# Hard-swish gates on GpSimd, later crossbar transposes and earlier weight loads in a fused top-k attention and feed-forward kernel

## The chip, the core and the metric

The kernel runs on one core of a Trainium2 chip. A core has five engines, each with a queue of its own that is worked off strictly in order: TensorE (PE in the profile; PEld is its weight load), VectorE (DVE), ScalarE (ACT), GpSimd (POOL) and SyncE (SP, which here only issues DMAs). An instruction waits on semaphores for what it needs from other engines, and while it waits, everything behind it on the same engine waits too. The metric is the device time of one execution in microseconds, lower is better; the figure of a kernel is the median of its runs.

## What is computed

Attention over 8 batches of 8 heads with 576 positions and 64 channels, in which each query keeps only its 32 largest scores; then a feed-forward block with a hard-swish between its two products, over the 4608 rows of all batches.

```python
scores = scale * np.matmul(q, k.transpose(0, 1, 3, 2))
kth = np.partition(scores, -top_k, axis=-1)[..., -top_k:-top_k + 1]     # top_k = 32
scores = np.where(scores >= kth, scores, -1000000000.0)
attn = np.exp(scores - np.max(scores, axis=-1, keepdims=True))
attn = attn / (np.sum(attn, axis=-1, keepdims=True) + 1e-09)
x = heads_joined(np.matmul(attn, v))                                    # 4608 x 512
h = x @ w_in                                                            # 512 x 2048
g = h * np.clip(h + 3.0, 0.0, 6.0) / 6.0
return g @ w_out                                                        # 2048 x 512
```

The feed-forward weights are float64 in memory; the kernel reads their raw words and makes float32 of them itself.

## The kernel before

**Attention, in duos.** The heads of a batch form four pairs, and two pairs at a time, for one tile of 128 queries, form a `Duo`. A batch has eight full duos (four query tiles, two halves of the heads) and two rest duos (the last 64 queries of each head): ten per batch, 80 in all. The main loop (L491) goes over them. A duo has two units, u = 0 and u = 1, one for each pair, and each unit of a full duo has two rows of tiles of 128 x 576 scores (a rest duo one). For each unit, VectorE finds the 32 largest scores of every query in four rounds (`top`, L238): MAX8 gives the next eight, MATCH_REPLACE8 strikes them out for the next round. `top(0)` to `top(3)` in the loop are the rounds of unit 0, `top(4)` to `top(7)` those of unit 1.

**What follows a unit's rounds.** `exp` (L254): GpSimd makes `kth`, the negated 32nd score, and a shift; ScalarE masks by a very steep Prelu (L265) and takes Exp with a running sum `den` (L270); GpSimd adds a constant to `den` (L275). `weights` (L277): VectorE inverts `den` (L284), GpSimd scales the scores (L287) and splits the float32 words into 16-bit halves, `e16` (L296). Then, still in `weights`, SP issues a transposing DMA of `e16` into `t16` (L299). `join` (L301): ScalarE puts the halves together into `eT` (L305). `values` (L313): TensorE multiplies by v, ScalarE copies the result into `xT` (L332). `exp(0)` and `weights(0)` of a duo come in its own step of the loop, `exp(1)` and `weights(1)` in the next, `join(0)` and `join(1)` in the next, `values` in the one after that. The scores of a duo are made one step ahead (`scores`, L195).

**Feed-forward, in pieces.** When the attention of 128 or 256 rows is complete, `queue` (L420) puts a `feed_forward` generator (L336) into `todo`. It is worked off in pieces between the steps of attention: a piece is either half of one 512-wide block of h (L349), at whose end ScalarE takes Relu(h + 3) into g (L357), or two products towards the output (L370), the last of which is followed by ScalarE's scaling by 1/6 (L380) and SP's store (L382). The gate, min(g, 6) * h, is one VectorE instruction (L361). It reads h from PSUM, and `piece` (L403) issues it two pieces after the piece that made g. The PSUM pool `ps_w` has three buffers for h, for the attention values and for the output sums; `ps_big` has one for scores and transposed inputs. At four places in each step (after rounds 0, 1, 3 and 5) `piece` is called with a count that depends on whether the duo is a rest duo and on the backlog `left`, in pieces (L496 to L500).

**Weights.** `convert` (L94) loads 128 x 512 raw float64 words into `st` (L100), then ScalarE (L105, L108), GpSimd (L106, L119) and VectorE (L114, L115) make float32 of them. There are 32 such chunks. `convert_step` (L462) is called after every round while chunks are left: it finishes an older chunk, then issues the load of the next one and starts on it at once.

**Buffers and queues.** The pool `kq` has 14 buffers of 4.6 KB per partition. Inputs as they land, transposed k and q, `st`, `e16`, `t16` and `eT` all come from it. Everything that SP issues goes through one queue, in the order of the program: input loads (L147, L151), values (L159, L163), weights (L100), transposes (L299) and stores (L382). The order is written out by hand; nothing reorders it.

Of the kernel before, what the change touches and what calls it, by code (L numbers as in the profile page):

```python
# [9 lines left out]
ALU = mybir.AluOpType  # L10
F32 = mybir.dt.float32
U32 = mybir.dt.uint32
I32 = mybir.dt.int32
U16 = mybir.dt.uint16
# [14 lines left out]
def kernel(  # L29
# [9 lines left out]
    nc = tc.nc  # L39
    P = nc.NUM_PARTITIONS  # L40
    B, H, S, D = q.shape
    DM, FF = moe_w_in.shape
    J = S // P
# [8 lines left out]
    def pool(name, bufs, **kw):  # L52
        return ctx.enter_context(tc.tile_pool(name=name, bufs=bufs, **kw))

    consts = pool("consts", 1)
    kqpool = pool("kq", 14)
    scpool = pool("sc", 3)
    wkpool = pool("wk", 1)
    mpool = pool("m", 4)
    xtpool = pool("xt", 2)  # L60
    xrpool = pool("xr", 1)
    gpool = pool("g", 8)
    opool = pool("o", 1)
    ps_big = pool("ps_big", 1, space=PSUM)
    ps_w = pool("ps_w", 3, space=PSUM)
# [28 lines left out]
    def convert(dst, src):  # L94

        st = kqpool.tile([P, 2 * WC], U32, tag="kq", name="st")
        nc.sync.dma_start(st[:], src)  # L100
        words = st[:].rearrange("p (n two) -> p n two", two=2)
        lo, hi = words[:, :, 0], words[:, :, 1]
        a = gpool.tile([P, WC], F32, tag="g", name="a")
        y = gpool.tile([P, WC], F32, tag="g", name="y")
        nc.scalar.activation(a[:], hi.bitcast(F32), AF.Abs)  # L105
        nc.gpsimd.tensor_scalar(a[:], a[:], HI_MOST, HI_LEAST, ALU.min, ALU.max)  # L106

        nc.scalar.activation(y[:], lo, AF.Copy, bias=2.0, scale=2.0**-51)  # L108
        yield

        au, yu = a[:].bitcast(U32), y[:].bitcast(U32)
        nc.vector.tensor_scalar(au, au, 3, None, ALU.logical_shift_left)  # L114
        nc.vector.scalar_tensor_tensor(  # L115
            out=yu, in0=hi, scalar=0x80000000, in1=yu,
            op0=ALU.bitwise_and, op1=ALU.bitwise_or,
        )
        nc.gpsimd.tensor_tensor(  # L119
            dst.bitcast(I32), a[:].bitcast(I32), y[:].bitcast(I32), ALU.add  # L120
        )
# [13 lines left out]
    class Pair:  # L135


        def __init__(self, b, hp):
            self.b, self.hp = b, hp
            self.vm, self.vr, self.kr = vms[hp], vrs[hp], krs[b % 2 * NHP + hp]  # L140
# [40 lines left out]
    class Duo:  # L181
# [6 lines left out]
        def __init__(self, pairs, qt):  # L188
            self.pairs, self.qt = pairs, qt
            self.rest = qt == J  # L190
            self.nt = 1 if self.rest else 2
            self.nb = J + 2 if self.rest else 2 * J + 1
            self.t16, self.eT = [None] * 2, [None] * 2

        def scores(self, us=(0, 1)):  # L195

# [80 lines left out]
        def weights(self, u):  # L277

            d = self.den[:, u, 0 : self.nt]
            nc.vector.reciprocal(d, d)  # L284
            for t in range(self.nt):
                row = self.row(u, t)
                nc.gpsimd.tensor_scalar(  # L287
                    row, row, self.den[:, u, t : t + 1], 1.0, ALU.mult, ALU.mult
                )
            n = self.nb * P  # L290
            e16 = kqpool.tile([P, 2 * (2 * J + 1) * P], U16, tag="kq", name="e16")
            halves = e16[:, 0 : 2 * n].rearrange("p (h x) -> p h x", h=2)
            parts = [(0, S + R, 0), (S - P, S, S + R)] if self.rest else [(0, n, 0)]
            for c0, c1, to in parts:
                words = self.sc[:, u, c0:c1].bitcast(U16).rearrange("p (x h) -> p h x", h=2)
                nc.gpsimd.tensor_copy(halves[:, :, to : to + c1 - c0], words)  # L296
            t16 = kqpool.tile([P, 2 * (2 * J + 1), P], U16, tag="kq", name="t16")
            self.t16[u] = t16
            nc.sync.dma_start_transpose(t16[:, 0 : 2 * self.nb, :], e16[:, 0 : 2 * n])  # L299

        def join(self, u):  # L301

# [33 lines left out]
    def feed_forward(xT, nt, rows):  # L336

        gs = []
        nf = 512 // nt
        for f0 in range(0, NFC, nf):
            h = ps_w.tile([P, 512], F32, tag="w", name="h")
            for f in range(f0, f0 + nf):
                if f == f0 + nf // 2:
                    yield None
                for i in range(NHP):
                    nc.tensor.matmul(  # L349
                        h[:, (f - f0) * nt : (f - f0 + 1) * nt],  # L350
                        w_in[:, i, f * P : (f + 1) * P],
                        xT[:, i, 0:nt],
                        start=(i == 0),
                        stop=(i == NHP - 1),
                    )
            g = gpool.tile([P, 512], F32, tag="g", name="g")
            nc.scalar.activation(g[:], h[:], AF.Relu, bias=three[:], scale=1.0)  # L357
            gs.append(g)

            def gate(g=g, h=h):  # L360
                nc.vector.scalar_tensor_tensor(  # L361
                    out=g[:], in0=g[:], scalar=6.0, in1=h[:], op0=ALU.min, op1=ALU.mult
                )

            yield gate
        for t0 in range(0, nt, P):
            acc = ps_w.tile([P, DM], F32, tag="w", name="acc")
            for f in range(NFC):
                c0 = f % nf * nt + t0
                nc.tensor.matmul(  # L370
                    acc[:],
                    gs[f // nf][:, c0 : c0 + P],
                    w_out[:, f, :],
                    start=(f == 0),
                    stop=(f == NFC - 1),
                )
                if f % 2 == 1:
                    if f == NFC - 1:
                        o = opool.tile([P, DM], F32, tag="o", name="o")
                        nc.scalar.mul(o[:], acc[:], 1.0 / 6.0)  # L380
                        for p0, p1, dst in rows(t0):
                            nc.sync.dma_start(dst, o[p0:p1, :])  # L382
                    yield None
# [16 lines left out]
    left = 0  # L400
# [56 lines left out]
            queue(state["xT"], c0 + P, rows)  # L457

    chunks = list(weight_chunks())
    converting = []  # L460

    def convert_step(depth=1):  # L462

        while len(converting) > depth:
            next(converting.pop(0), None)
        if converting and not chunks:
            next(converting.pop(0), None)
        if chunks:
            c = convert(*chunks.pop(0))
            next(c)  # L470
            converting.append(c)

    def pair_at(m, first):

# [2 lines left out]

    first = pairs[0]
    first[0].load()
    convert_step(2)  # L480
    first[0].transpose()
    duos[0].scores((0,))
    first[1].load()
    convert_step(2)
    first[1].transpose()
    duos[0].scores((1,))
    first[2].load()
    convert_step(2)
    first[3].load()

    for m in range(ND + 2):  # L491
        u = duos[m] if m < ND else None
        prev = duos[m - 1] if 0 < m <= ND else None


        level = (left >= 10) + (left >= 20)  # L496
        if u and u.rest:
            count = [(1, 0, 1, 0), (1, 0, 1, 1), (1, 1, 1, 1)][level]
        else:
            count = [(2, 1, 2, 1), (2, 2, 2, 1), (2, 2, 2, 2)][level]  # L500
        depth = 2 if m < 2 else 1

        def top(r):
            if u:
                u.top(r // 4, r % 4)
            convert_step(depth)

        if prev:
            prev.exp(1)
        elif m == 0:  # L510
            first[2].transpose()
            first[3].transpose()
        if m + 1 < ND:
            duos[m + 1].scores()
        top(0)
        piece(count[0])
        p = pair_at(m, 4)
        if p:
            p.load()
        if m == 0:  # L520
            first[0].load_values()
            first[1].load_values()
        top(1)
        if prev:
            prev.weights(1)
        if m > 1:
            values(m - 2)
        if u and u.pairs[0].b and 1 <= m % per_batch <= 2:
            for p in duos[m - 1].pairs:
                p.load_values()  # L530
        piece(count[1])
        top(2)
        if prev:
            prev.join(0)
        top(3)
        if u:
            u.exp(0)
        if m == 0:
            first[2].load_values()
            first[3].load_values()  # L540
        piece(count[2])
        top(4)
        p = pair_at(m, 5)
        if p:
            p.transpose()
        top(5)
        if u:
            u.weights(0)
        piece(count[3])
        top(6)  # L550
        if prev:
            prev.join(1)
        top(7)
        if m == 3:
            piece(3)
    while todo:
        piece()
    piece(2)
# [33 lines left out]
```

## Time and profile before

| | |
|---|---|
| Median of three runs | 1792.3 us (1792.1 to 1793.2) |
| The profiled execution | 1793.5 us, of which its instructions span 1791.7 us |
| Granted TensorE clock, mean over the span | 0.923 |
| MAX8 and MATCH_REPLACE8 on VectorE, mean of one | 744 and 740 ns |
| The gate L361 on VectorE | 144 times, 96.7 us, 106.4 us of idle time before it |
| Relu L357 on ScalarE | 144 times, 97.1 us |
| Matmuls towards h (L349) and towards the output (L370) | 474.8 us for 2304 records, 523.4 us for 1152 |
| Transposing DMA L299, issue to landing | 160 times, 4.6 us |
| Weight load L100, issue to landing | 32 times, 5.2 us |

In the profile a line such as `L361 DVE SCALAR_TENSOR_TENSOR g<-g,h` names the line of the kernel, the engine, the operation and what it writes and reads; then come shapes, count, busy time, mean time of one, and the time for which the engine stood idle just before, with what ended the wait. A float32 matmul leaves two records. In a timeline, the first column is the start in us from the beginning of the span and the second the time taken; `SPq` is SP's queue, where the time is that from the first issue to the last of a merged row.

### The profile page before, as it was taken

To read this page: it belongs to the slowest core of one execution; us is meant where nothing else is said; L and a number is where in the kernel's file an instruction comes from. 1 tells how busy PE (TensorE), PEld (TensorE's weight loads), DVE (VectorE), ACT (ScalarE), POOL (GpSimd) and SP (SyncE) were. 2 spreads that over 40 slices of the span, in tenths; PEclk is the share of its full clock that TensorE was granted. 3 is DMA by queue.
4 is the path that set the end of the run, shared out by engine and by line. 5 is a ranking of instruction groups with operands and counts; after the bars stand their busy time and mean duration, and the time that the engine had idled before them with its cause. 6 is when DMAs were issued, how large, how long until landed. Compare 5 with 4: busy or idle time off the path is not lost.

```text
span 1791.7 us, 24696 instructions
## 1 busy us (share of the span) xinstructions
PE 1502.2 (84%) x8480; PEld 986.7 (55%) x8480; DVE 1560.9 (87%) x3249; ACT 1190.7 (66%) x1639; POOL 735.2 (41%) x1218
## 2 busy tenths in 40 slices
PE   5122767697999999899999899899999899998999
PEld 2012454464665656464756656565666565555575
DVE  3856899999999989999999989999999999999310
ACT  4354687777877777678777777777766877766410
POOL 2565444434444444444344444434443434444100
PEclk9555888799999999999999999999999999999999
DMA  6323343444344433535244442444244533323200
GB/s 184 90 92 121 90 100 63 80 85 92 71 82 88 92 83 54 102 78 109 49 79 90 80 88 49 108 86 91 54 101 82 92 64 73 83 54 70 46 13 12
DMA packets 450302, 144.23 MB, mean 80 GB/s; under 512 B 433280, under 2 KB 441472, under 8 KB 450176
## 3 DMA queue, kind: packets, MB, share of 16 engines
q1 hardware_dynamic: 450176, 142.65, 37.9%
q8 instruction: 67, 1.10, 0.3%
q14 instruction: 59, 0.48, 0.1%
HBM read 45.09 MB, written 9.44 MB: 30 GB/s over the span
## 4 chain that ended last, share of the span: by engine, by line
DVE 64%; PE 14%; ACT 12%; POOL 3%; issue 3%; DMA 3%; SPq 0%; ACTq 0%; POOLq 0%
DVE m L245 32%; DVE wk L249 26%; PE acc L370 7%; DVE g L361 4%; PE h L349 4%; ACT eT L305 3%; ACT sc L270 3%; ACT sc L228 2%; PE big L222 2%; ACT sc L265 2%; PE pv L325 1%; DMA st<-in_moe_w_out_dram 1%; DMA t<-e 1%; DMA st<-in_moe_w_in_dram 1%; POOL a L106 1%
## 5 line engine op out<-in xcount | busy, mean ns | idle before, releaser
L245 DVE MAX8 m<-wk 128x8 f32<-128x576 f32 x864 | 612.5, 744 | 2.0
L370 PE MATMUL acc<-w_out,g 128*128 128x512 f32 x1152 | 523.4, 602 | 6.2 <-DVE g L361 6.2
L349 PE MATMUL h<-xT,w_in 128*128 128x256 f32 (+1 forms) x2304 | 474.8, 364 | 33.6 <-DVE g L361 22.2
L349 PEld LDWEIGHTS h<-xT,w_in 128*128 128x128 f32 x2304 | 402.6, 195 | 90.9 <-issue 19.1
L305 ACT COPY eT<-t 128x2304 uint16<-128x2304 uint16 (+1 forms) x160 | 418.4, 2615 | 39.6 <-DMA t<-e 39.3
L249 DVE MATCH_REPLACE8 wk<-m,wk 128x576 f32<-128x576 f32 x576 | 423.1, 740 | 0.0
L265 ACT ACTIVATE sc<-sc,kth 128x576 f32<-128x576 f32 x288 | 209.1, 768 | 252.3 <-POOL kth L260 252.2
L370 PEld LDWEIGHTS acc<-w_out,g 128*128 128x128 f32 x1152 | 213.2, 192 | 240.0 <-issue 229.3
L296 POOL COPY e<-sc 128x2304 uint16<-128x2304 uint16 (+1 forms) x192 | 321.2, 1683 | 10.1
L287 POOL TENSOR_SCALAR sc<-sc,den 128x576 f32<-128x576 f32 x288 | 214.7, 754 | 269.4 <-DVE den L284 263.9
L325 PE MATMUL pv<-eT,vm 128*64 128x128 f32 (+1 forms) x2560 | 182.2, 285 | 127.2 <-ACT eT L305 87.6
L325 PEld LDWEIGHTS pv<-eT,vm 128*64 128x64 f32 x2560 | 148.1, 148 | 178.0 <-ACT eT L305 93.0
L270 ACT ACTIVATE sc<-sc,shift 128x576 f32<-128x576 f32 x288 | 219.2, 762 | 3.0
L275 POOL TENSOR_SCALAR den<-den 128x2 f32<-128x2 f32 (+1 forms) x160 | 35.5, 222 | 446.8 <-ACT sc L270 446.8
L245 DVE MAX8 m<-sc 128x8 f32<-128x576 f32 x288 | 203.3, 742 | 15.6 <-ACT sc L231 15.6
L249 DVE MATCH_REPLACE8 wk<-m,sc 128x576 f32<-128x576 f32 x288 | 211.5, 740 | 0.0
L222 PE MATMUL big<-kq 64*128 64x512 f32 x512 | 144.0, 685 | 73.9 <-ACT kr L179 34.6
L361 DVE SCALAR_TENSOR_TENSOR g<-g,h 128x512 f32<-128x512 f32 x144 | 96.7, 672 | 106.4 <-ACT g L357 106.2
L357 ACT ACTIVATE g<-h,three 128x512 f32<-128x512 f32 x144 | 97.1, 681 | 88.0 <-PE h L349 87.8
L222 PEld LDWEIGHTS big<-kq 64*128 64x128 f32 x512 | 48.6, 206 | 142.0 <-issue 46.4
L228 ACT COPY sc<-big 128x2048 f32<-128x2048 f32 (+1 forms) x65 | 118.4, 1822 | 11.2 <-PE big L225 10.9
L260 POOL TENSOR_SCALAR kth<-m 128x2 f32<-128x2 f32 (+1 forms) x160 | 36.5, 228 | 116.9 <-DVE m L245 116.4
(45 smaller groups left out, 996.6 us busy)
## 6 DMA issues: line engine op xcount, KB each, us to landing
landed<-in_k_dram SPq DMA_DIRECT2D x64, 128.0 KB, 2.8
landed<-in_q_dram SPq DMA_DIRECT2D x64, 128.0 KB, 2.9
st<-in_moe_w_in_dram SPq DMA_DIRECT2D x16, 512.0 KB, 5.2
vm<-in_v_dram SPq DMA_DIRECT2D x64, 128.0 KB, 2.3
st<-in_moe_w_out_dram SPq DMA_DIRECT2D x16, 512.0 KB, 5.2
out_dram<-o SPq DMA_DIRECT2D x32, 256.0 KB, 2.4
t<-e SPq DMA_TRANSPOSE x160, 4.6
landed<-in_k_dram SPq DMA_DIRECT2D x32, 32.0 KB, 2.6
```

The costliest lines, as they stand in the source:

```text
L222: nc.tensor.matmul(banks[:, 2 * i + hh, :], pr.qT[d, qs], pr.kT[d, :])
L245: nc.vector.max(self.m[:, t, 8 * r : 8 * r + 8], self.cur[t])
L249: nc.vector.match_replace(wk, self.m[:, t, 8 * r : 8 * r + 8], self.cur[t], LOWEST)
L265: nc.scalar.activation(row, row, AF.Prelu, bias=kth[:, t : t + 1], scale=1.0, alpha=STEEP)
L270: nc.scalar.activation(row, row, AF.Exp, bias=shift[:, t : t + 1], scale=scale, accum_out=self.den[:, u, t : t + 1],)
L287: nc.gpsimd.tensor_scalar(row, row, self.den[:, u, t : t + 1], 1.0, ALU.mult, ALU.mult)
L296: nc.gpsimd.tensor_copy(halves[:, :, to : to + c1 - c0], words)
L305: nc.scalar.copy(eT[:, 0 : self.nb, :] .rearrange("p c q -> p (c q)") .bitcast(U16) .rearrange("p (x h) -> p h x", h=2), self.t16[u][:, 0 ...
L325: nc.tensor.matmul(pv[hh * D : (hh + 1) * D, u * w : (u + 1) * w], pr.vm[:, hh, c, :] if c < J else pr.vr[:, hh, :], rhs, start=(c == 0), ...
L349: nc.tensor.matmul(h[:, (f - f0) * nt : (f - f0 + 1) * nt], w_in[:, i, f * P : (f + 1) * P], xT[:, i, 0:nt], start=(i == 0), stop=(i == NH ...
L361: nc.vector.scalar_tensor_tensor(out=g[:], in0=g[:], scalar=6.0, in1=h[:], op0=ALU.min, op1=ALU.mult)
L370: nc.tensor.matmul(acc[:], gs[f // nf][:, c0 : c0 + P], w_out[:, f, :], start=(f == 0), stop=(f == NFC - 1),)
```

## The change

Five things are changed.

1. The gate is two GpSimd instructions, a minimum and a product, instead of one on VectorE. GpSimd reads h from SBUF, so ScalarE makes a copy `hs` of h right after the Relu; it comes from a new pool `h` with two buffers. `kq` has 13 buffers for 14.
2. The transposing DMA is no longer issued at the end of `weights` but in a method of its own, `flip`. For unit 1 it is called after round 3 instead of after round 1, for unit 0 after round 7 instead of after round 5.
3. `convert` stops once more, right after it has issued its load. A list `landing` holds chunks that are loaded and not yet begun, `land` issues loads, and `convert_step` finishes one chunk, begins one and issues one load. At the start two weight loads follow the inputs of the first two pairs, where one load followed each pair.
4. The backlog has four levels with thresholds at 10, 18 and 26, where it had three at 10 and 20, and the highest issues ten pieces in a full duo and six in a rest duo (eight and four before).
5. The three extra pieces after the fourth duo are gone.

```diff
-    kqpool = pool("kq", 14)
+    kqpool = pool("kq", 13)
...
+    hpool = pool("h", 2)
...
         nc.sync.dma_start(st[:], src)
+        yield
...
-            t16 = kqpool.tile([P, 2 * (2 * J + 1), P], U16, tag="kq", name="t16")
-            self.t16[u] = t16
-            nc.sync.dma_start_transpose(t16[:, 0 : 2 * self.nb, :], e16[:, 0 : 2 * n])
+            self.e16[u] = e16
+
+        def flip(self, u):
+            t16 = self.t16[u] = kqpool.tile([P, 2 * (2 * J + 1), P], U16, tag="kq", name="t16")
+            n = 2 * self.nb
+            nc.sync.dma_start_transpose(t16[:, 0:n, :], self.e16[u][:, 0 : n * P])
...
             nc.scalar.activation(g[:], h[:], AF.Relu, bias=three[:], scale=1.0)
+            hs = hpool.tile([P, 512], F32, tag="h", name="hs")
+            nc.scalar.copy(hs[:], h[:])
             gs.append(g)
-            def gate(g=g, h=h):
-                nc.vector.scalar_tensor_tensor(
-                    out=g[:], in0=g[:], scalar=6.0, in1=h[:], op0=ALU.min, op1=ALU.mult
-                )
+            def gate(g=g, hs=hs):
+                nc.gpsimd.tensor_scalar(g[:], g[:], 6.0, 1.0, ALU.min, ALU.mult)
+                nc.gpsimd.tensor_tensor(g[:], g[:], hs[:], ALU.mult)
...
-    converting = []
-
-    def convert_step(depth=1):
-
-        while len(converting) > depth:
-            next(converting.pop(0), None)
-        if converting and not chunks:
-            next(converting.pop(0), None)
-        if chunks:
+    landing, converting = [], []
+
+    def land(count=1):
+
+        for _ in range(min(count, len(chunks))):
             c = convert(*chunks.pop(0))
             next(c)
+            landing.append(c)
+
+    def convert_step(depth=2):
+
+        if len(converting) >= depth or not landing:
+            for c in converting[:1]:
+                next(c, None)
+            del converting[:1]
+        if landing:
+            c = landing.pop(0)
+            next(c)
             converting.append(c)
+        land()
...
     first[0].load()
-    convert_step(2)
+    first[1].load()
+    land(2)
     first[0].transpose()
     duos[0].scores((0,))
-    first[1].load()
-    convert_step(2)
+    convert_step()
+    first[2].load()
     first[1].transpose()
     duos[0].scores((1,))
-    first[2].load()
-    convert_step(2)
+    convert_step()
     first[3].load()
+    land()
...
-        level = (left >= 10) + (left >= 20)
+        level = (left >= 10) + (left >= 18) + (left >= 26)
         if u and u.rest:
-            count = [(1, 0, 1, 0), (1, 0, 1, 1), (1, 1, 1, 1)][level]
+            count = [(1, 0, 1, 0), (1, 1, 1, 1), (1, 1, 1, 1), (2, 1, 2, 1)][level]
         else:
-            count = [(2, 1, 2, 1), (2, 2, 2, 1), (2, 2, 2, 2)][level]
-        depth = 2 if m < 2 else 1
+            count = [(2, 1, 2, 1), (2, 2, 2, 1), (2, 2, 2, 2), (3, 2, 3, 2)][level]
...
         top(3)
+        if prev:
+            prev.flip(1)
...
         top(7)
-        if m == 3:
-            piece(3)
+        if u:
+            u.flip(0)
```

More of the change, by code (lines that the diff above doesn't have):

```diff
@@ L192, in __init__ @@
             self.nb = J + 2 if self.rest else 2 * J + 1
-            self.t16, self.eT = [None] * 2, [None] * 2
+            self.e16, self.t16, self.eT = [None] * 2, [None] * 2, [None] * 2
         def scores(self, us=(0, 1)):
@@ L505, in top @@
                 u.top(r // 4, r % 4)
-            convert_step(depth)
+            convert_step()
         if prev:
```

## The prediction, made before the changed kernel was run

> **What bounds the kernel now.** I read the totals first, then the busy time by stage, then the timelines of three places: the weight conversion at the start, one duo in the middle, and the end.
>
> ```profile
> PE 1502.2 (84%) x8480; PEld 986.7 (55%) x8480; DVE 1560.9 (87%) x3249; ACT 1190.7 (66%) x1639; POOL 735.2 (41%) x1218
> ```
>
> Two engines are near the span, so averages don't say which one sets the time. Three stretches of 50 us from the view by stages (busy us of PE, PEld, DVE, ACT, POOL, then clock, DMA share, GB/s) do:
>
> ```profile
> 100.00:150.00 50.00, 9.20 (x52) 5.71 (x52) 28.25 (x47) 22.54 (x32) 29.39 (x34) 0.53 0.36 107
> 1150.00:1200.00 50.00, 46.61 (x260) 35.34 (x259) 50.00 (x108) 35.96 (x53) 18.34 (x32) 0.97 0.41 85
> 1700.00:1750.00 50.00, 50.00 (x307) 38.10 (x306) 5.50 (x8) 6.70 (x10) 0.00 (x0) 1.00 0.03 11
> ```
>
> So there are three stages: a start in which nothing is full, a middle in which VectorE is full, and an end in which only TensorE works. From the first MAX8 of each duo in the DVE timeline: duos 0 to 3 run from 16.4 to 199.8 us, duos 4 to 79 from there to 1668.8, and the rest (122.9 us) is feed-forward left over.
>
> The start, by the timelines of SP, ACT, POOL and DVE:
>
> ```profile
> 107.04 2.68 SPq L299 DMA_TRANSPOSE t<-e  x1
> 109.83 1.97 SPq L100 DMA_DIRECT2D st<-in_moe_w_out_dram  x4
> ...
> 113.81 0.66 ACT L105 ACTIVATE a<-st 128x512 f32<-128x512 f32 x1 [12.37 <-DMA st<-in_moe_w_out_dram]
> ...
> 114.56 0.61 POOL L106 TENSOR_SCALAR a<-a 128x512 f32<-128x512 f32 x1 [5.88 <-ACT a L105]
> ...
> 115.21 1.48 DVE L114 TENSOR_SCALAR a<-a 128x512 uint32<-128x512 uint32 x1 [5.19 <-POOL a L106]
> ```
>
> Read upward: DVE waits for POOL, POOL for ACT, ACT for a weight load, which SP issued only after the transpose ahead of it, and that waited for its input e16. DVE idles 57 us this way in duos 0 to 3: 10.8 in duo 0, 46.4 in duos 1 to 3.
>
> The middle: half a duo on DVE, and the same half on POOL in a duo with four gates.
>
> ```profile
> 902.89 1.40 DVE L245 MAX8 m<-sc 128x8 f32<-128x576 f32 x2
> ...
> 912.60 1.39 DVE L245 MAX8 m<-sc 128x8 f32<-128x576 f32 x2
> ```
>
> ```profile
> 783.33 0.22 POOL L260 TENSOR_SCALAR kth<-m 128x2 f32<-128x2 f32 x1 [1.04 <-DVE m L245]
> ...
> 786.62 0.22 POOL L275 TENSOR_SCALAR den<-den 128x2 f32<-128x2 f32 x1 [2.61 <-ACT sc L270]
> 789.55 1.47 POOL L287 TENSOR_SCALAR sc<-sc,den 128x576 f32<-128x576 f32 x2 [2.71 <-DVE den L284]
> 791.08 2.10 POOL L296 COPY e<-sc 128x2304 uint16<-128x2304 uint16 x1
> ```
>
> A half takes DVE 9.70, a duo 19.40, plus 0.60 for every gate (20.00, 20.60, 21.20, 21.80 with 1 to 4). A rest duo takes 12.67. POOL's own chain in a half is 3.5 us from kth to the end of den, then 1.5 and 2.1: 7.1, so 14.2 a duo. A rest duo has one tile per half, and its rows make 2.3 + 1.1 + 1.6 = 5.0, so 10.0.
>
> **The change, part by part.** *Gates off DVE.* 144 gates of 0.60 go; 127 stand in duos 4 to 79 (I stepped through the counts in the code). DVE's floor there is 61 x 19.40 + 15 x 12.67 = 1373.5 us; with its 127 gates 1449.7, measured 1469.0.
>
> *Gates on POOL.* No row shows an f32 product of this size on POOL. Nearest:
>
> ```profile
> L119 POOL TENSOR_TENSOR w_in<-a,y 128x512 int32<-128x512 int32 x16 | 22.0, 1378 | 0.2
> L106 POOL TENSOR_SCALAR a<-a 128x512 f32<-128x512 f32 x32 | 21.2, 662 | 80.3 <-ACT a L105 79.8
> ```
>
> The minimum is L106's operation: 0.61 at its median. The product lies between 0.61 (if two inputs cost no more than one) and L119's worst, 1.70; L119's median is 1.27, the same shape with two inputs, so I take it. A gate is then 1.9, with ends 1.2 and 2.5 (0.79 + 1.70). POOL runs in order: behind a gate wait kth, so ACT's Prelu and Exp, so den and DVE's reciprocal (L284), which stands 5.6 us into a half while den is ready at 3.5; and the e16 copy, the transpose and the join. So gates in one half lengthen POOL's chain to 7.1 + 1.9 each, and two per half (10.9) exceed DVE's 9.7. Stepping the new counts through gives, of 61 full duos, 24 with no gate, 11 with 1, 6 with 2, 6 with 3, 11 with 4, 3 with 5; of 15 rest duos 8 with 3 and 3 with 2. Excess of 14.2 + 1.9 g over 19.40: 6 x 0.5 + 11 x 2.4 + 3 x 4.3 = 42.3; of 10.0 + 1.9 g over 12.67: 8 x 3.0 + 3 x 1.1 = 27.6. DVE and POOL together: 1373.5 + 69.9 = 1443.
>
> The Trainium skill speaks against this move (GPSIMD Engine Reference, section "Engine selection": elementwise work belongs on VectorE, two inputs being some 2x slower on GPSIMD); the trace agrees in kind, 0.67 for the whole gate on DVE against 1.9, but DVE is the full engine here. The 4497 ns for 2048 elements in its section "Elementwise — side-by-side cycle accounting" would make the product 1.12 (an estimate), the gate 1.74, and the sum 1426 instead of 1443.
>
> *A second copy of h.* 144 ACT copies of 128x512 out of PSUM; the nearest row, L380, is 0.60, so 86 us. ACT spends 242.8 us in the middle waiting for kth (L265 <- L260); the copies lie in that. If this cover is gone they delay Exp one for one. In return the PSUM tile is free after ACT and no longer after a gate: in the waits of 400 to 1665 us PE lost 23.2 (values), 11.8 (h) and 5.9 (acc) to L361. Those 41 us go, which TensorE now needs.
>
> *TensorE.* A piece is (411.3 + 63.5 + 63.1 + 523.4) / 576 = 1.84 by its rows, 1.77 in a stream; I take 1.82. With 5.2 for the attention of a full duo, 3.7 of a rest duo and 1.15 for a transposed pair, the old counts give 1317 for duos 4 to 79, where 1305 were busy. The new counts put 519 pieces there for 501: 1349. That is near DVE's floor, and uneven: ten pieces make 23.4 and more, six 16.1. If no lag may carry from duo to duo, DVE and PE give 1449; if 6 us may, 1403. The longest of the three engines, duo by duo without carry, gives 1476. POOL's excess and PE's fall on the same duos, so I take 1450.
>
> *Pieces at a backlog.* Before, 16 pieces in the last two steps and 52 after them: 68 x 1.82 = 123.8, measured 122.9. Now 20 + 33 = 53: 96.5.
>
> *The start.* Weight loads now lead by three steps (at least 8.5 us against 5.2 to land), and SP reaches each transpose two rounds later, when e16 is done. That takes the 46.4 of duos 1 to 3. Duo 0's 10.8 stays, since ACT is held there by the score copies; putting the first conversions later also costs a round in duo 0. DVE's conversion work stays at 59 us, but L114 runs 1.49 instead of 0.42 beside a busy POOL, and POOL gets denser; I give back 10. Gain 36, ends 0 and 46.
>
> *Transposes later in the middle.* One of each duo's two passes, on SP, an output store and in 14 duos eight value loads (4.7 us of issue at 749.46 to 754.14); these loads wait for PE to finish with the old values. Joins follow 7 us after e16, a transpose lands in 4.6: 2.4 of cover, against loads that start earlier and so spare PE's 15.6 us of waiting for vm. I take 0; the bounds are 14 x 2.3 = 32 lost and 16 gained. Thirteen kq buffers for 14: fifteen weight loads wait for the slot just read by DVE, hidden by the three steps; without that cover, the old idle returns.
>
> **The sum.** 16.4 to the first MAX8, 183.4 - 36 = 147.4 for duos 0 to 3, 1450, 96.5: span 1710. The profiled execution spans 1791.7 (1793.5 in all); the median of the runs, 1792.3, is 0.6 above that span. Predicted 1711.
>
> **Rivals.** (1) Lags carry over, POOL's waits hide beside DVE, and DVE sets the pace: 1403 for the middle, 1664 in all. For it: PE's 41 us of gate waits disappear. Against: two gates exceed a half on POOL.
> (2) POOL becomes the bound, and the kernel slower. The place is the gate between den and the scaling L287; the price is 1534 for the middle at 2.5 per gate, which is 1795, and 10 us more per tenth above; at 2.8 it makes 1828. It decides from 2.5. For it: L119 reaches 1.70, and each gate also waits for ACT's copy and so for PE. Against: contention stretched L119 only where DVE ran conversions, which end before the middle.
> (3) The start stays: slots and queue take back what the earlier loads give. 1711 + 36 = 1747. For it: kq loses a buffer while three more loads are out; against: the loads need the slot three steps early.
>
> **How the numbers follow.** Forecast 0.50, (1) 0.22, (3) 0.10, (2) 0.18. About 0.2% is what a measurement here tells from no change. Only (2) reaches no change or slower: 0.03 within, 0.15 slower, so 0.82 faster. The range 1650 to 1800 takes in a full start gain and DVE's pace below (16 + 137 + 1403 + 95), and 2.5 per gate above.
>
> **What would show it.** The two POOL lines of a gate at 0.6 and 1.3 us; DVE busy near 1464; POOL near 1006; ACT no longer waiting for weights; duos of four gates near 21.8, without gates 19.4; some 97 us after the last MAX8. It is wrong if reciprocals wait long in duos without gates, if POOL's products take over 1.9, or if duos 0 to 3 still take 180.

## The result

The changed kernel takes 1888.6 us at the median of its runs, against 1792.2 us for the kernel before in the same session: 1.0538 times as long, with a 95% interval of 1.0520 to 1.0557. It is slower by 5.4%, where 4.5% faster was forecast. The profiled execution took 1889.9 us and spans 1888.1.

### The profile after

The totals of the changed kernel, and the groups that answer to those shown of before (busy us, mean ns of one | idle us just before):

```profile
PE 1542.6 (82%) x8480; PEld 997.7 (53%) x8480; DVE 1478.1 (78%) x3105; ACT 1263.4 (67%) x1783; POOL 1202.2 (64%) x1506
...
L368 POOL TENSOR_SCALAR g<-g 128x512 f32<-128x512 f32 x144 | 278.9, 1937 | 50.5 <-ACT g L362 39.8
...
L286 DVE RECIPROCAL den<-den 128x2 f32<-128x2 f32 (+1 forms) x160 | 25.7, 161 | 277.8 <-POOL den L277 277.5
...
L369 POOL TENSOR_TENSOR g<-g,hs 128x512 f32<-128x512 f32 x144 | 183.4, 1274 | 12.0
```

The reciprocal in the kernel before, its two shapes apart:

```profile
L284 DVE RECIPROCAL den<-den 128x2 f32<-128x2 f32 x128 | 19.7, 154 | 25.3 <-POOL den L275 25.2
L284 DVE RECIPROCAL den<-den 128x1 f32<-128x1 f32 x32 | 5.1, 158 | 16.9 <-POOL den L275 16.9
```

VectorE has lost 83 us of work, and the waiting in front of a reciprocal that itself takes 0.16 has grown from 42 to 278 us. GpSimd has gained 467 us, of which 279 are the minimum L368: it takes 1.94 us, and 0.61 had been predicted from another instruction of the same operation and shape.

The changed kernel by stages (the cuts are the first MAX8 of duo 4 and the end of the last MAX8; columns as before):

```profile
0.00:156.00 156.00, 61.08 (x337) 41.62 (x338) 124.11 (x212) 87.68 (x141) 101.04 (x130) 0.79 0.53 151
156.00:1788.00 1632.00, 1385.37 (x7569) 887.81 (x7569) 1353.79 (x2893) 1150.23 (x1604) 1058.47 (x1345) 0.92 0.36 73
1788.00:1889.00 101.00, 96.19 (x577) 68.29 (x575) 0.17 (x1) 25.47 (x39) 42.69 (x31) 0.99 0.10 23
```

The middle of the kernel before:

```profile
200.00:1669.00 1469.00, 1324.88 (x7588) 867.56 (x7584) 1425.10 (x3020) 1080.98 (x1470) 630.70 (x1078) 0.96 0.40 80
```

The start ends at 156 us where it ended at 200, and the end is 101 us long where it was 123. Both gains came about. The middle went from 1469 to 1632 us, and there no engine is full: VectorE, the third column of busy times, works 83% of it, where it worked 97%. TensorE's granted clock over the middle is lower too, 0.92 for 0.96, but that is not what VectorE waits for: 273 of its 278 us without work in this stretch are waits for GpSimd's den.

Half a duo in this middle, with a gate in both places where one can stand (behind den and behind the split into e16), from the POOL timeline of the changed kernel (start, us taken, operation, idle time before it):

```profile
1469.88 0.23 POOL L262 TENSOR_SCALAR kth<-m 128x2 f32<-128x2 f32 x1
...
1473.18 0.22 POOL L277 TENSOR_SCALAR den<-den 128x2 f32<-128x2 f32 x1 [2.60 <-ACT sc L272]
1473.48 1.94 POOL L368 TENSOR_SCALAR g<-g 128x512 f32<-128x512 f32 x1
1475.50 1.29 POOL L369 TENSOR_TENSOR g<-g,hs 128x512 f32<-128x512 f32 x1
1476.78 1.48 POOL L289 TENSOR_SCALAR sc<-sc,den 128x576 f32<-128x576 f32 x2
1478.32 2.10 POOL L298 COPY e<-sc 128x2304 uint16<-128x2304 uint16 x1
1480.51 1.93 POOL L368 TENSOR_SCALAR g<-g 128x512 f32<-128x512 f32 x1
1482.52 1.27 POOL L369 TENSOR_TENSOR g<-g,hs 128x512 f32<-128x512 f32 x1
1483.76 0.23 POOL L262 TENSOR_SCALAR kth<-m 128x2 f32<-128x2 f32 x1
```

From one kth to the next 13.88 us pass, and but for gaps of 0.1 or less GpSimd is idle only for the 2.6 us until ScalarE has taken Prelu and Exp. VectorE's half takes 9.70. So the gate behind the split delays the next kth, kth delays Prelu, Exp and den, and VectorE waits at the reciprocal, as its own timeline shows:

```profile
1473.44 0.17 DVE L286 RECIPROCAL den<-den 128x2 f32<-128x2 f32 x1 [4.07 <-POOL den L277]
...
1476.29 1.41 DVE L247 MAX8 m<-wk 128x8 f32<-128x576 f32 x2
...
1487.32 0.17 DVE L286 RECIPROCAL den<-den 128x2 f32<-128x2 f32 x1 [4.08 <-POOL den L277]
```

VectorE is done with the last MAX8 of a unit at 1477.70, and the kth made from it starts at 1483.76. 9.70 + 4.1 is GpSimd's 13.9 but for 0.1, and two such halves take 27.8 us for VectorE's 19.4. That is the loss in small: 14.2 us of chain a duo, plus 3.3 for every gate, as far as that exceeds what VectorE needs.

### The profile page after: what moved, and what is told of

It is laid out like the page before. It is cut to its first block, busy times and chain, and to the rows that moved or that the text cites. A ratio compares the mean times of both kernels' runs of the same rounds, so it can differ in the third digit from the quotient of the medians.

```text
span 1888.1 us, 25153 instructions
## 1 busy us (share of the span) xinstructions
PE 1542.6 (82%) x8480; PEld 997.7 (53%) x8480; DVE 1478.1 (78%) x3105; ACT 1263.4 (67%) x1783; POOL 1202.2 (64%) x1506
## 4 chain that ended last, share of the span: by engine, by line
POOL 37%; DVE 29%; ACT 15%; PE 12%; issue 6%; DMA 1%; SPq 1%; POOLq 0%; ACTq 0%
DVE m L247 16%; POOL g L368 12%; DVE wk L251 12%; POOL e L298 8%; ACT sc L272 7%; POOL g L369 7%; PE acc L376 6%; POOL sc L289 5%; ACT sc L267 4%; PE h L354 3%; PE pv L330 1%; POOL kth L262 1%; POOL den L277 1%; ACT eT L310 1%; PE big L224 1%
## 5 line engine op out<-in xcount | busy, mean ns | idle before, releaser
L376 PE MATMUL acc<-w_out,g 128*128 128x512 f32 x1152 | 541.1, 619 | 36.4 <-POOL g L368 23.3
L354 PE MATMUL h<-xT,w_in 128*128 128x256 f32 (+1 forms) x2304 | 498.1, 375 | 62.6 <-ACT hs L364 44.6
L354 PEld LDWEIGHTS h<-xT,w_in 128*128 128x128 f32 x2304 | 414.9, 201 | 130.3 <-ACT hs L364 49.8
L376 PEld LDWEIGHTS acc<-w_out,g 128*128 128x128 f32 x1152 | 219.4, 198 | 286.7 <-issue 236.8
L298 POOL COPY e<-sc 128x2304 uint16<-128x2304 uint16 (+1 forms) x192 | 321.3, 1683 | 10.2
L368 POOL TENSOR_SCALAR g<-g 128x512 f32<-128x512 f32 x144 | 278.9, 1937 | 50.5 <-ACT g L362 39.8
L330 PE MATMUL pv<-eT,vm 128*64 128x128 f32 (+1 forms) x2560 | 169.2, 278 | 92.8 <-ACT eT L310 92.7
L286 DVE RECIPROCAL den<-den 128x2 f32<-128x2 f32 (+1 forms) x160 | 25.7, 161 | 277.8 <-POOL den L277 277.5
L330 PEld LDWEIGHTS pv<-eT,vm 128*64 128x64 f32 x2560 | 137.4, 143 | 142.3 <-ACT eT L310 104.4
L369 POOL TENSOR_TENSOR g<-g,hs 128x512 f32<-128x512 f32 x144 | 183.4, 1274 | 12.0
```

Of the source, the lines that this page charges most:

```text
L330: nc.tensor.matmul(pv[hh * D : (hh + 1) * D, u * w : (u + 1) * w], pr.vm[:, hh, c, :] if c < J else pr.vr[:, hh, :], rhs, start=(c == 0), ...
L354: nc.tensor.matmul(h[:, (f - f0) * nt : (f - f0 + 1) * nt], w_in[:, i, f * P : (f + 1) * P], xT[:, i, 0:nt], start=(i == 0), stop=(i == NH ...
L368: nc.gpsimd.tensor_scalar(g[:], g[:], 6.0, 1.0, ALU.min, ALU.mult)
L369: nc.gpsimd.tensor_tensor(g[:], g[:], hs[:], ALU.mult)
L376: nc.tensor.matmul(acc[:], gs[f // nf][:, c0 : c0 + P], w_out[:, f, :], start=(f == 0), stop=(f == NFC - 1),)
```

## The experiments

All but e4, which runs the forms by themselves, have the shape of one of the two kernels; the labels e1 to e9 are those that the expectations use. "The middle" is duos 4 to 79, from the first MAX8 of duo 4 to the end of the last.

### The other form of the minimum (e1)

```diff
-                nc.gpsimd.tensor_scalar(g[:], g[:], 6.0, 1.0, ALU.min, ALU.mult)
+                nc.gpsimd.tensor_scalar(g[:], g[:], 6.0, 0.0, ALU.min, ALU.max)
```

> One change to the changed kernel: the first GpSimd instruction of the gate is (min 6, max 0) instead of (min 6, times 1); g is a Relu and so not negative, and the value stays the same. Theory A, the pair min-times-1 is a slow form on GpSimd (1.94 us) while L106's min-max of the same shape takes 0.61: the gate falls from 3.2 to 1.9 us, the waits of the reciprocal from 277 us to under 90, the middle (duos 4 to 79) from 1631 to 1450 to 1480 us, and the whole to 1705 to 1735 us, faster than both. Theory B, any gate in GpSimd's order between den and the scaling costs the chain, whatever its form: the reciprocal's waits stay above 200 us and the time above 1800. Theory C, the product or data in g makes it slow: L368 stays at 1.9 us and the time at 1888.

Measured 1733.3 us, 0.968 of before (0.966 to 0.970): 155 us less than the changed kernel, by a change of one operation and its constant. Theory A holds.

```profile
L368 POOL TENSOR_SCALAR g<-g 128x512 f32<-128x512 f32 x144 | 88.8, 617 | 63.5 <-ACT g L362 53.0
```

The middle takes 1478 us, and its granted clock is 0.96 again. The reciprocal still waits 126 us in all, more than the 90 that were expected.

### Gates back on VectorE (e2)

```diff
-            hs = hpool.tile([P, 512], F32, tag="h", name="hs")
-            nc.scalar.copy(hs[:], h[:])
...
-            def gate(g=g, hs=hs):
-                nc.gpsimd.tensor_scalar(g[:], g[:], 6.0, 1.0, ALU.min, ALU.mult)
-                nc.gpsimd.tensor_tensor(g[:], g[:], hs[:], ALU.mult)
+            def gate(g=g, h=h):
+                nc.vector.scalar_tensor_tensor(
+                    out=g[:], in0=g[:], scalar=6.0, in1=h[:], op0=ALU.min, op1=ALU.mult
+                )
```

> The changed kernel with its gates on VectorE as before, without the copy of h and its pool; later transposes, earlier loads, four backlog levels and 13 buffers stay. Theory A, the gates alone lost the time: duos 0 to 3 end near 156 us as in the changed kernel, the middle takes VectorE's 1373 + 131 x 0.6 = 1452 and some 20 to 35 us of waits, the end 100: 1725 to 1745 us. Theory D, the later transposes or the ten pieces of the highest level cost time in the middle too: over 1792.

Measured 1734.4 us, 0.969 (0.967 to 0.971). Theory A: everything else in the change together gains 3.1%. The start ends at 156.5 us, the middle takes 1480, the end 95. That is also the time of the fast form on GpSimd (e1): in this order of work the move of the gates, by itself, gains nothing.

### The gates alone (e3)

The kernel before, with only the gates of the changed kernel, their copy of h and 13 buffers.

> The kernel before with the gates of the changed kernel (GpSimd, copy of h, 13 buffers) and nothing else. Theory A: duos 0 to 3 stay at 183 us, the middle is the sum over its duos of the longer of VectorE (19.4, 12.67), GpSimd (14.2 or 10.0 and 3.2 per gate) and TensorE, 1556 to 1565 and some 20 more, the end 123: 1880 to 1910 us. Theory D: clearly under 1850, since part of the loss would be the other edits'.

Measured 1948.4 us, 1.088 (1.086 to 1.090): slower than both, and 38 us over the upper end of what A gave. Theory D is out. The start ends at 199.5, as before; the middle takes 1614 and the end 131. The sum over duos had 1565 without what a delay hands on to the next duo; how much of the missing 49 us is that was not tried.

### Thirteen forms on GpSimd (e4)

```python
v.tensor_scalar(x[:], x[:], 6.0, 1.0, ALU.min, ALU.mult)     # L53
v.tensor_scalar(x[:], x[:], 6.0, 0.0, ALU.min, ALU.max)
v.tensor_scalar(x[:], x[:], 1.0, 1.0, ALU.mult, ALU.mult)
v.tensor_scalar(x[:], x[:], 1.0, 6.0, ALU.mult, ALU.min)
v.tensor_scalar(x[:], x[:], 0.0, 1.0, ALU.max, ALU.mult)
v.tensor_scalar(x[:], x[:], 0.0, 6.0, ALU.max, ALU.min)
v.tensor_scalar(x[:], x[:], 6.0, 0.0, ALU.min, ALU.add)
v.tensor_scalar(x[:], x[:], 0.0, 1.0, ALU.add, ALU.mult)
v.tensor_scalar(x[:], x[:], 6.0, None, ALU.min)
v.tensor_scalar(y[:], x[:], 6.0, 1.0, ALU.min, ALU.mult)
v.tensor_scalar(x[:], x[:], six[:, 0:1], one[:, 0:1], ALU.min, ALU.mult)
v.tensor_tensor(x[:], x[:], w[:], ALU.mult)
v.tensor_tensor(x[:], x[:], w[:], ALU.add)                   # L65
```

> Nothing but thirteen GpSimd forms on a 128x512 float32 tile, six times each, alone on the chip; the whole computation is left out. Theory A: min-times takes 1.9 us as in the kernel, min-max and max-min 0.6, times-times 0.6, the product of two tiles 1.27. Theory C (it is the data, the place or the neighbours): min-times takes 0.6 here. Open: whether times-min, max-times, min-plus and a lone min are fast.

The groups of this kernel by line (busy us, mean ns of one):

```profile
L63 POOL TENSOR_SCALAR x<-x,six,one 128x512 f32<-128x512 f32 x6 | 12.4, 2068 | 0.6
L56 POOL TENSOR_SCALAR x<-x 128x512 f32<-128x512 f32 x6 | 11.6, 1932 | 0.5
L59 POOL TENSOR_SCALAR x<-x 128x512 f32<-128x512 f32 x6 | 11.6, 1928 | 0.5
L57 POOL TENSOR_SCALAR x<-x 128x512 f32<-128x512 f32 x6 | 11.6, 1927 | 0.5
...
L58 POOL TENSOR_SCALAR x<-x 128x512 f32<-128x512 f32 x6 | 11.5, 1919 | 0.5
L53 POOL TENSOR_SCALAR x<-x 128x512 f32<-128x512 f32 x6 | 11.5, 1918 | 1.5 <-DVE x L46 1.0
L61 POOL TENSOR_SCALAR x<-x 128x512 f32<-128x512 f32 x6 | 8.9, 1488 | 0.5
L64 POOL TENSOR_TENSOR x<-x,w 128x512 f32<-128x512 f32 x6 | 7.6, 1261 | 0.5
L65 POOL TENSOR_TENSOR x<-x,w 128x512 f32<-128x512 f32 x6 | 7.6, 1259 | 0.5
L55 POOL TENSOR_SCALAR x<-x 128x512 f32<-128x512 f32 x6 | 3.7, 618 | 0.5
L60 POOL TENSOR_SCALAR x<-x 128x512 f32<-128x512 f32 x6 | 3.7, 617 | 0.5
L54 POOL TENSOR_SCALAR x<-x 128x512 f32<-128x512 f32 x6 | 3.7, 612 | 0.5
```

Alone on the chip, with other data and no neighbour, min-times takes 1.92 us: theory C is out. Three of the pairs tried are fast (min-max, times-times, plus-times, all near 0.62), the others take three times as long, among them max-min, the same pair the other way round, which had been expected at 0.6; a lone minimum is at 1.49. Why one pair is fast and another slow, no run shows.

### Transposes at the old place (e5)

The kernel with gates on VectorE, with its transposes issued at the end of `weights` again.

```diff
             self.e16[u] = e16
+            self.flip(u)
...
-        if prev:
-            prev.flip(1)
...
-        if u:
-            u.flip(0)
```

> The kernel with gates on VectorE (e2) and its transposes issued at the end of weights again, as before; the loads still lead by three steps. Theory G, the lead of the loads alone ended the idle time of the start: duos 0 to 3 still end within 5 us of 156, the time within 10 us of 1734. Theory H, the later place in SP's queue is what frees the loads: duos 0 to 3 end at 175 us or later and the time is 1750 or more.

Measured 1736.1 us, 0.969 (0.967 to 0.970); the start ends at 156.6 and the middle takes 1479. Theory G: the later place in SP's queue is worth nothing, neither in the start nor in the middle. The moved gates with 13 buffers don't shorten the start either (199.5 in e3), and with the three old levels it still ends at 155.9 (e6). What remains is the loads' lead of three steps, with their new order at the very start; the three extra pieces after the fourth duo, which are gone as well, were not put back by themselves.

### The three old levels (e6)

```diff
-        level = (left >= 10) + (left >= 18) + (left >= 26)
+        level = (left >= 10) + (left >= 20)
...
-            count = [(1, 0, 1, 0), (1, 1, 1, 1), (1, 1, 1, 1), (2, 1, 2, 1)][level]
+            count = [(1, 0, 1, 0), (1, 0, 1, 1), (1, 1, 1, 1)][level]
...
-            count = [(2, 1, 2, 1), (2, 2, 2, 1), (2, 2, 2, 2), (3, 2, 3, 2)][level]
+            count = [(2, 1, 2, 1), (2, 2, 2, 1), (2, 2, 2, 2)][level]
```

> The kernel with gates on VectorE (e2) and the three old backlog levels (10, 20; eight pieces at most). Theory I, the ten pieces only move TensorE's work: the end after the last MAX8 grows from 95 to 115 to 120 us, the middle shrinks from 1480 to 1455 to 1465, and the time stays within 8 us of 1734. Theory J, they shorten the whole: over 1745 without them. Theory K, they overfill TensorE: under 1722 without them.

Measured 1753.9 us, 0.979 (0.977 to 0.981), so theory J: the levels gain about 20 us beside gates on VectorE. The end grows from 95 to 123 us without them, and the middle shrinks only from 1480 to 1472; I had expected 1455 to 1465. Work put into the middle comes at 8 us there for 28 at the end. What is left against the kernel before, 38 us, is then the start, which ends 44 us earlier; the middle is 3 us longer than before and the end the same.

### Gates in GpSimd's gaps (e7 and e8)

The kernel with the fast form; gates that come due after rounds 1 and 5 are held back and issued in the next `exp`, between the shift and den. Those after rounds 0 and 3, between den and the scaling, stay where they are. The pool of the copy of h has three buffers for two.

```diff
-    hpool = pool("h", 2)
+    hpool = pool("h", 3)
...
+            while late:
+                late.pop(0)()
             d = self.den[:, u, 0:nt]
             nc.gpsimd.tensor_scalar_add(d, d, EPS)
...
-                if gate:
+                if gate and hold:
+                    late.append(gate)
+                elif gate:
                     gate()
...
-        piece(count[1])
+        piece(count[1], True)
...
-        piece(count[3])
+        piece(count[3], True)
```

> The kernel with the fast form (e1), and gates that come due after rounds 1 and 5 put behind the shift of the next exp, ahead of den, where GpSimd stands idle for 2.6 us until ScalarE's Exp is done; three buffers for the copy of h. Theory L, what is left of the reciprocal's waits (126 us in e1) is a gate of 1.9 us ahead of kth or of the scaling, in a half whose chain is already 7.1 us: the waits fall under 70 us, the middle from 1478 to 1400 to 1450, and the time to 1655 to 1705. Theory M, TensorE is the bound of the middle by now: the waits move to VectorE's waiting for other things and the time stays above 1715.

Measured 1683.8 us, 0.940 (0.938 to 0.941), theory L, except that the reciprocal's waits, 73.9 us, stay a little above the 70 expected. In this version some gates of the loop's last two steps come behind the products that read g, so that these products read a g that has not been gated; hence the next run, in which only duos hold gates back:

```diff
-        piece(count[1], True)
+        piece(count[1], u is not None)
...
-        piece(count[3], True)
+        piece(count[3], u is not None)
```

> As e7, but gates are held back for the next exp only while the loop still has duos; in its last two steps, where no exp follows, they are issued at once. Theory L: the same time as e7 within 3 us, 1681 to 1687 us. Theory N, e7's gain comes from what it left undone in its last two steps: over 1700.

Measured 1681.0 us, 0.938 (0.936 to 0.940): theory L again, and faster than both kernels. A half with two gates, from its POOL timeline, with the scaling of the next half, which has only one:

```profile
926.22 0.21 POOL L264 TENSOR_SCALAR shift<-shift 128x2 f32<-128x2 f32 x1
926.51 0.61 POOL L370 TENSOR_SCALAR g<-g 128x512 f32<-128x512 f32 x1
927.21 1.28 POOL L371 TENSOR_TENSOR g<-g,hs 128x512 f32<-128x512 f32 x1
929.05 0.22 POOL L279 TENSOR_SCALAR den<-den 128x2 f32<-128x2 f32 x1 [0.55 <-ACT sc L272]
929.34 0.61 POOL L370 TENSOR_SCALAR g<-g 128x512 f32<-128x512 f32 x1
930.04 1.27 POOL L371 TENSOR_TENSOR g<-g,hs 128x512 f32<-128x512 f32 x1
931.37 1.47 POOL L291 TENSOR_SCALAR sc<-sc,den 128x576 f32<-128x576 f32 x2
...
938.74 0.22 POOL L279 TENSOR_SCALAR den<-den 128x2 f32<-128x2 f32 x1 [0.55 <-ACT sc L272]
941.07 1.47 POOL L291 TENSOR_SCALAR sc<-sc,den 128x576 f32<-128x576 f32 x2 [2.10 <-DVE den L288]
```

One gate fills the wait for ScalarE's Exp and leaves 0.55 of its 2.6 us; the other fills the wait for the reciprocal, and the scaling starts 2.3 us after den with it or without it. The reciprocal's waits fall from 126 to 76.6 us and the middle from 1478 to 1426. How much of that is the third buffer was not tried; in e1 ScalarE stood idle for 10.0 us in all until a buffer for the copy came free, and in e8 not at all.

### A third instruction in the gate (e9)

```diff
                 nc.gpsimd.tensor_scalar(g[:], g[:], 6.0, 0.0, ALU.min, ALU.max)
+                nc.gpsimd.tensor_scalar(g[:], g[:], 1.0, 1.0, ALU.mult, ALU.mult)
```

> The kernel with the fast form (e1) and a third GpSimd instruction in each gate, times 1 times 1 on g, which takes 0.62 us alone; the value stays the same. A gate is then 2.5 us, where the prediction put the point at which GpSimd's chain makes the kernel as slow as before. Theory A, time follows the length of the gate alone: the sum over the duos at 2.5 is 1534, and the whole, between e1's 1733 at 1.9 and 1889 at 3.2, 1785 to 1805 us. Theory B, it is the number of GpSimd instructions or the slow form itself: under 1760 or over 1830.

Measured 1810.3 us, 1.010 (1.008 to 1.012), 5 us above the range of A. A gate of e1, with what follows it on GpSimd:

```profile
1232.72 0.61 POOL L368 TENSOR_SCALAR g<-g 128x512 f32<-128x512 f32 x1
1233.41 1.27 POOL L369 TENSOR_TENSOR g<-g,hs 128x512 f32<-128x512 f32 x1
1234.67 1.48 POOL L289 TENSOR_SCALAR sc<-sc,den 128x576 f32<-128x576 f32 x2
```

And one of this kernel, with the start of the next:

```profile
1054.71 0.61 POOL L368 TENSOR_SCALAR g<-g 128x512 f32<-128x512 f32 x1
1055.40 0.62 POOL L369 TENSOR_SCALAR g<-g 128x512 f32<-128x512 f32 x1
1056.10 1.27 POOL L370 TENSOR_TENSOR g<-g,hs 128x512 f32<-128x512 f32 x1
1057.46 0.61 POOL L368 TENSOR_SCALAR g<-g 128x512 f32<-128x512 f32 x1
```

From the start of one gate to the next instruction GpSimd takes 1.95 us in the fast kernel, 2.75 here and 3.30 in the changed one, since each step of a gate also starts some 0.08 after the end of the one before it; so this gate was longer than the 2.5 I had reckoned from the instructions' own times. The three times, 1733, 1810 and 1889, rise with it, by 96 and then 142 us for each further microsecond of gate. Not the number of instructions decides (three of them are faster than the two slow ones), but their time in the queue. On the line between the first two, the time of the kernel before is reached at some 2.55 us, or some 2.35 counted by the instructions' own times, as the prediction counts.

## Why the prediction was wrong

**The step that failed** is the price of the minimum: "The minimum is L106's operation: 0.61 at its median", and with it the upper end of a gate, 2.5, made from the worst of two fast rows. Engine, operation name, type and shape were the same; the second arithmetic operation was not, times 1 for max. It measured 1.94. The row I took was one of the three fast pairs, and so was the row behind L287 (times-times): the kernel before held no slow one of this size, and its trace could not show that there are any. A bound from the nearest rows excluded what none of them had. What an unseen pair costs should have been left open upwards, or the range not cut at 1800.

The Trainium skill's accounting would have supported the same mistake (GPSIMD Engine Reference, section "Elementwise — side-by-side cycle accounting": a loop body of up to two operations takes 1.03 cycles per element). At the page's 1.2 GHz that is an estimate of 0.44 us for 512 elements, before what an instruction costs once. L54 of e4, 0.61 us, is near it; L53, two operations as well, takes three times L54's time, and the measurement decides.

**The chain was right.** Priced at 1.9 per gate, the sum of the longest of three engines without carry gave 1476 for the middle; the kernel with the fast form has 1478. At 2.5 it gives 1534, and e9 has 1553; priced at 3.2, it gives 1612, and the changed kernel has 1632. I had chosen 1450 instead of 1476 with the words that GpSimd's excess and TensorE's fall on the same duos. The 1476 takes that in already, being the longest of the three for each duo, and these three middles lie above the sum and not below it. So the 26 us taken off had no ground.

**Rival 2** was this outcome, and near in its price and its point of turning: 10 us for each tenth of a microsecond of gate, where the runs give 12.6 and then 11.1 by the instructions' own times, and 2.5 us, where the line through two runs gives some 2.35. Its place was half of it: it named the gate between den and the scaling, but in the half shown the gate ahead of kth costs as much of the queue, and e8 leaves the first where it is while the middle falls by 52 us. Its reason was wrong (contention and waiting for the copy of h: the product kept its 1.27, and GpSimd waited 40 us in all for ScalarE in front of gates), and its chance of 0.18 too small for that reason's sake.

**The other terms.** The product L369 at 1.27 is exact, the copy of h took 0.58 for 0.60, VectorE's busy time 1478 for 1464. The start gained 43 us for 36, without the 10 I gave back for contention. The end took 100 us for 96.5. The move of the transposes was put at 0 and is worth nothing; but in the start I credited SP's later transposes beside the loads, and e5 has the same gain without them. The 41 us in which TensorE waited for gates did not become free: between 400 and 1665 us of the changed kernel it waits for the copy of h, for the transposed keys and for GpSimd (us in all, times, longest).

```profile
PE big L212 <- ACT kr L181: 38.9, 6, 10.3
PE h L354 <- ACT hs L364: 37.2, 10, 6.5
...
PE acc L376 <- POOL g L368: 14.3, 3, 4.8
PE acc L376 <- POOL g L369: 7.6, 2, 3.8
```

## What to carry to other kernels

Price an instruction by a row with the same pair of operations in the same order, not by its name and shape; where there is none, leave the upper end open, and measure the pair alone before the rest is built on it. When work moves to an engine that is half idle, add it to that engine's chain between two fixed waits, not to its busy time: here gates of 1.9 us filled waits that were there anyway in two places of the queue; with some of them in two other places the kernel took some 50 us longer (and had one buffer fewer for the copy of h). The second engine gained nothing from taking the work (1733 us against 1734) until its order had room for it.

## What was not expected of the hardware

On GpSimd, a two-operation TENSOR_SCALAR on 128x512 float32 takes 0.61 to 0.62 us for min-max, times-times and plus-times, and 1.92 to 1.93 for min-times, times-min, max-times, max-min and min-plus. Min-times into another tile has a mean of 1922 ns; with its scalars read from SBUF it takes 0.15 more; and a minimum without a second operation takes 1.49, more than the fast pairs of two. So a second operation that changes nothing (max 0 on values that are not negative) makes a minimum faster. And beside the changed kernel's busier GpSimd, VectorE's MAX8 and MATCH_REPLACE8 kept their time (746 and 742 ns where they had 744 and 740). That doesn't hold for all of VectorE's work: in the weight conversion of the same run its shift L116 takes 0.41 us with GpSimd idle, and up to 1.50 beside GpSimd's addition L121 and 1.81 beside its copy L298.
